# A linear-attention and mixer-MLP kernel on one core: its head reordered (held-back DMA transposes, PE transposes in two PSUM tiles, K chunks finished one by one) and LN1 applied in the Q stage

## The chip, the cores and the metric

The kernel runs on one core of one Trainium2 chip. The metric is the device time of one execution in microseconds (us). A program on one core has no second core to compare with, so every run is read next to runs of the kernel before on the same chip; all runs in this document count as fast ones. PE is the TensorE matmul engine, PEld its weight load, DVE VectorE, ACT ScalarE, POOL GpSimd, SP SyncE (which issues most DMAs).

## The reference, cut to what matters

```python
# x: (1, 2048, 640) bf16; 32 heads of 20
g = sigmoid((x * gate_w).sum(-1, keepdims=True))
# A: linear attention
q, k, v = split_heads(x @ wqkv)
phi = lambda t: where(t > 0, t + 1, exp(t)) + 1e-6
o = phi(q) @ (phi(k)^T v) / (phi(q) . sum(phi(k)) + 1e-6)      # per head
a = merge_heads(o) @ wo
# B: mixer
h  = gelu(layernorm(x) @ w1)                                   # LN1
x1 = x + shift_quarters(h) @ w2
b  = x1 + gelu(layernorm(x1) @ w3) @ w4
out = g * a + (1 - g) * b
```

## The kernel before

Tokens come in 16 chunks of 128. The stages, in PE's order, are: a *head*, in which x chunks 0 to 2 are transposed on PE (the others come transposed by DMA) and multiplied with the K weights; the *K stage*, in which each chunk's K becomes `pk = phi(K)` and is multiplied into the product G = x^T pk; the *Q stage* (ten Q groups, with the rest of G between them); then `w1`, `kv`, `w2`, `w3`, `w4`. PSUM is four tiles `PP[0..3]` of 1024 f32 columns, used in halves of 512, and handed round by `alloc` and `release` in first-in first-out order.

Loads and POOL's work, in program order (cut):

```python
for dc in (0, 1, 2, 4):
    load_wk(aq, dc)                      # K weights, issued from ACT
load_x(0, 1); load_x(1, 2); load_x(2, 3) # plain x chunks, issued from SP
load_wk(sp, 3)
load_xT(3, 4)                            # DMA transposes from here on
load_xT(4, 5); load_x(3, 4); load_xT(5, 7); load_x(4, 6); load_xT(7, 9)
load_x(6, 9); load_xT(9, 12); load_x(9, 12); load_xT(12, 16); load_x(12, 16)
sp.dma_start(wq, ...); sp.dma_start(w1, ...); sp.dma_start(wv, ...)   # [cut: wo6, w2]
# [cut: POOL memsets and masks]
for g in range(4):                       # POOL: waits for the load of w1
    nc.gpsimd.tensor_copy(w1x4[:, :, g, :], w1g[:, :, g, P:CG])
```

phi, LN1 and the head:

```python
def ln1_sq(c):                           # sum of squares on ACT, every 4th chunk the rest on POOL
    act(junk[:], x_sb[:, c, :], ACT.Square, accum_out=sq[:, c:c + 1])
    if c % 4 == 3:
        ...                              # [cut: four small POOL operations: me, ve, sq, ve]
        nc.gpsimd.tensor_tensor(rs1[:, g], ve[:, g], nhalf[:], op=ALU.pow)

def ln1_apply(c):                        # DVE, then a DMA transpose into lnxT
    nc.vector.tensor_scalar(lx[:], x_sb[:, c, :], me[:, c:c + 1], rs1[:, c:c + 1], ...)
    sp.dma_start_transpose(lnxT[:, :, c * P:(c + 1) * P], lx[:])

def phi(dst, src, n, extra=None):        # one ACT exp, two DVE operations
    act(e[:, 0:n], src, ACT.Exp)
    if extra is not None: act(extra[0], extra[1], ACT.Copy)
    nc.vector.tensor_scalar(e[:, 0:n], e[:, 0:n], 1.0, 1e-6, op0=ALU.min, op1=ALU.add)
    nc.vector.scalar_tensor_tensor(dst, src, 0.0, e[:, 0:n], op0=ALU.max, op1=ALU.add)  # L272

for _ in range(5):                       # warm-up
    mm(PP[3][:, 512:1024], lhsT=warm[:, 0:P], rhs=warm[:], start=True, stop=True)
tb = [PP[3][:, 0:512].bitcast(BF16), PP[3][:, 512:1024].bitcast(BF16)]

def x_tr(c, b):
    for dc in range(DC):
        nc.tensor.transpose(tb[b][:, dc * P:(dc + 1) * P], x_sb[:, c, dc * P:(dc + 1) * P], ident[:])
    v = tb[b][:, 0:DC * P].rearrange("p (j s) -> p j s", j=DC)
    nc.vector.tensor_copy(xT[:, 0:3, c * P:(c + 1) * P], v[:, 0:3])
    act(xT[:, 3:5, c * P:(c + 1) * P], v[:, 3:5], ACT.Copy)

x_tr(0, 0)
nc.tensor.transpose(tb[1][:, 0:DC], g5[0:DC, :], ident[0:DC, 0:DC])    # the gate row
for dc in range(DC):
    nc.vector.tensor_copy(wkg[:, dc, D:D + 1], tb[1][:, dc:dc + 1])    # 5 small copies
x_tr(1, 1)
k_mm(0, 0, 0); k_mm(0, 0, 1)
x_tr(2, 0)
k_mm(1, 1, 0); k_mm(1, 1, 1); k_mm(2, 2, 0); k_mm(2, 2, 1)
for dc in range(2, DC):
    for c in range(3):
        k_mm(c, c, dc)
        if dc == DC - 1:
            k_post(c, c)                 # phi, release
for c in range(3, NCH):                  # K stage
    p = alloc()
    for dc in range(DC): k_mm(c, p, dc)
    k_post(c, p)
    g_unit(0, c - 3)
    if c % 2 == 0: pop(ln1_s)
    if c >= 12:    pop(ln1_a)            # LN1 apply of chunks 0 to 3
```

Of the kernel before, what the change touches and what calls it, by code (L numbers as in the profile page):

```python
# [8 lines left out]
ACT = mybir.ActivationFunctionType  # L9
ALU = mybir.AluOpType  # L10
BF16 = mybir.dt.bfloat16
# [5 lines left out]
def kernel(  # L17
# [13 lines left out]
    nc = tc.nc  # L31
    P = 128
    S, D = A_x.shape[1], A_x.shape[2]
# [3 lines left out]
    DC = D // P  # L37
    GW = 120
    gsz = [GW] * 5 + [D - 5 * GW]
# [3 lines left out]
    CG = D // 4  # L43
# [4 lines left out]
    out2 = out.rearrange("b s d -> (b s) d")  # L48
# [4 lines left out]
    def sb(name, cols, dt=BF16):  # L53
        return const.tile([P, cols], dt, name=name)
# [7 lines left out]
    xT = RXT[:].rearrange("p (j s) -> p j s", j=DC)  # L62
# [7 lines left out]
    x_sb = RXH[:, 0:NCH * D].rearrange("p (c d) -> p c d", c=NCH)  # L70
# [4 lines left out]
    wkg = RA[:, 0:DC * KP].rearrange("p (j d) -> p j d", j=DC)  # L75
    o_ = DC * KP
    wq = RA[:, o_:o_ + DC * D].rearrange("p (j d) -> p j d", j=DC)
    o_ += DC * D
    wv = RA[:, o_:o_ + DC * D].rearrange("p (j d) -> p j d", j=DC)
    w3 = RA[:, 0:DC * F].rearrange("p (j f) -> p j f", j=DC)  # L80
    w1 = RB[:, 0:DC * D].rearrange("p (j d) -> p j d", j=DC)
    wo6 = RB[:, DC * D:DC * D + 6 * D].rearrange("p (g d) -> p g d", g=6)
# [3 lines left out]
    w2 = sb("w2", DC * D)[:].rearrange("p (j d) -> p j d", j=DC)  # L86
# [13 lines left out]
    w1x = sb("w1x", DC * P)[:].rearrange("p (j d) -> p j d", j=DC)  # L100
    kvT = sb("kvT", 6 * GW)[:].rearrange("p (g d) -> p g d", g=6)
    warm = sb("warm", 512)
    ident = sb("ident", P)
    ones32 = sb("ones32", 32)
    c32 = sb("c32", 1)
    mask4 = sb("mask4", P)
    mask32 = mask4[:, 0:32]
    E4 = sb("E4", P)
    bmask = sb("bmask", GW, F32)
    g5 = sb("g5", P)  # L110
# [23 lines left out]
    PP = [psum.tile([P, 1024], F32, name=f"pp{i}") for i in range(4)]  # L134
    free = [0, 1, 2, 3]

    def alloc():
        return free.pop(0)

    def release(i):  # L140
        free.append(i)

    mm = nc.tensor.matmul
    act = nc.scalar.activation
# [5 lines left out]
    sp, aq = nc.sync, nc.scalar  # L150
    xv = x2.rearrange("(c p) d -> p c d", p=P)

    def load_x(c0, c1):
        sp.dma_start(x_sb[:, c0:c1, :], xv[:, c0:c1, :])  # L154

    def load_xT(c0, c1):
        sp.dma_start_transpose(xT[:, :, c0 * P:c1 * P], x2[c0 * P:c1 * P, :])  # L157
# [5 lines left out]
    def load_wk(q, dc):  # L163
        q.dma_start(wkg[:, dc, 0:D], A_wqkv[dc * P:(dc + 1) * P, D:2 * D])
# [4 lines left out]
    load_x(1, 2)  # L169
    load_x(2, 3)  # L170
    load_wk(sp, 3)
    load_xT(3, 4)
    load_xT(4, 5)
    load_x(3, 4)
    load_xT(5, 7)
    load_x(4, 6)
    load_xT(7, 9)
    load_x(6, 9)
    load_xT(9, 12)
    load_x(9, 12)  # L180
    load_xT(12, 16)
    load_x(12, 16)
    rows = lambda w, a, b: w[:, a:b].rearrange("(j p) d -> p j d", p=P)
    sp.dma_start(wq, rows(A_wqkv, 0, D))
    sp.dma_start(w1, rows(B_w1, 0, D))
    sp.dma_start(wv, rows(A_wqkv, 2 * D, 3 * D))
    sp.dma_start(wo6[0:GW, 0:5, :], A_wo[0:5 * GW, :].rearrange("(g r) d -> r g d", r=GW))
    sp.dma_start(wo6[0:gsz[5], 5, :], A_wo[5 * GW:D, :])
    sp.dma_start(w2[:, 0:4, :], B_w2.rearrange("(g c) d -> c g d", c=CG)[0:P])
    for g in range(4):  # L190
        sp.dma_start(w2[32 * g:32 * (g + 1), 4, :], B_w2[CG * g + P:CG * (g + 1), :])


    for dc in range(DC):
        nc.gpsimd.memset(wkg[:, dc, D + 1:D + 2], 1.0)
    nc.gpsimd.memset(ones32[:], 1.0)
# [5 lines left out]
                            pattern=[[-DH, 6], [0, DH]], channel_multiplier=1)  # L202
    nc.gpsimd.affine_select(out=bm3, in_=bm3, compare_op=ALU.is_ge, fill=0.0, base=DH - 1,
                            pattern=[[DH, 6], [0, DH]], channel_multiplier=-1)
    nc.gpsimd.memset(mask4[:], 1.0)
    m4 = mask4[:].rearrange("p (f h) -> p f h", f=4)
    nc.gpsimd.affine_select(out=m4, in_=m4, compare_op=ALU.is_ge, fill=0.0, base=0,
                            pattern=[[0, 4], [-4, 32]], channel_multiplier=1)
    nc.gpsimd.affine_select(out=m4, in_=m4, compare_op=ALU.is_ge, fill=0.0, base=3,
                            pattern=[[0, 4], [4, 32]], channel_multiplier=-1)  # L210
    nc.gpsimd.memset(hsT[:, :, 0:4], 0.0)
    nc.gpsimd.memset(hsT[:, :, S:S + 4], 0.0)
    w1g = w1.rearrange("p k (g c) -> p k g c", c=CG)
    w1x4 = w1x.rearrange("p k (g c) -> p k g c", g=4)
    for g in range(4):
        nc.gpsimd.tensor_copy(w1x4[:, :, g, :], w1g[:, :, g, P:CG])


    def stats(mv, c, src):
# [35 lines left out]
    ln1_a = [lambda c=c: ln1_apply(c) for c in range(NCH)]  # L255

    def pop(q, n=1):
        for _ in range(n):
            if q:
                q.pop(0)()  # L260
# [13 lines left out]
    def k_mm(c, p, dc):  # L274
        for (n0, n1) in ((0, 512), (512, KW)):
            mm(PP[p][:, n0:n1], lhsT=xT[:, dc, c * P:(c + 1) * P], rhs=wkg[:, dc, n0:n1],  # L276
               start=(dc == 0), stop=(dc == DC - 1))

    def k_post(c, p):
        phi(pk[:, c, :], PP[p][:, 0:D], D, (ym[:, c, :], PP[p][:, D:D + 2]))  # L280
        release(p)
# [6 lines left out]
    def g_post(i, p):  # L288
        act(Gp[:, i, :], PP[p][:, 0:D], ACT.Copy)
        release(p)  # L290
# [3 lines left out]
    def g_unit(i, c):  # L294
        if c == 0:
            gp[0] = alloc()
        g_step(i, c, gp[0])
        if c == NCH - 1:
            g_post(i, gp[0])


    for _ in range(5):
        mm(PP[3][:, 512:1024], lhsT=warm[:, 0:P], rhs=warm[:], start=True, stop=True)
    tb = [PP[3][:, 0:512].bitcast(BF16), PP[3][:, 512:1024].bitcast(BF16)]

    def x_tr(c, b):
        for dc in range(DC):
            nc.tensor.transpose(tb[b][:, dc * P:(dc + 1) * P], x_sb[:, c, dc * P:(dc + 1) * P], ident[:])
        v = tb[b][:, 0:DC * P].rearrange("p (j s) -> p j s", j=DC)
        nc.vector.tensor_copy(xT[:, 0:3, c * P:(c + 1) * P], v[:, 0:3])  # L310
        act(xT[:, 3:5, c * P:(c + 1) * P], v[:, 3:5], ACT.Copy)

    for _ in range(3):
        alloc()
    x_tr(0, 0)
    nc.tensor.transpose(tb[1][:, 0:DC], g5[0:DC, :], ident[0:DC, 0:DC])
    for dc in range(DC):
        nc.vector.tensor_copy(wkg[:, dc, D:D + 1], tb[1][:, dc:dc + 1])
    x_tr(1, 1)
    k_mm(0, 0, 0)  # L320
    k_mm(0, 0, 1)
    x_tr(2, 0)
    k_mm(1, 1, 0)
    k_mm(1, 1, 1)
    k_mm(2, 2, 0)
    k_mm(2, 2, 1)
    for dc in range(2, DC):
        for c in range(3):
            k_mm(c, c, dc)
            if dc == DC - 1:  # L330
                k_post(c, c)


    for c in range(3, NCH):
        p = alloc()
        for dc in range(DC):
            k_mm(c, p, dc)
        k_post(c, p)
        g_unit(0, c - 3)
        if c % 2 == 0:  # L340
            pop(ln1_s)
        if c >= 12:
            pop(ln1_a)


    gq = [(0, c) for c in range(NCH - 3, NCH)] + [(i, c) for i in range(1, DC) for c in range(NCH)]
    wqp = wq.rearrange("p k (q j) -> p k j q", j=DC)

    def z_rows():
        p = alloc()  # L350
        nc.tensor.transpose(PP[p][:, 0:64].bitcast(BF16), mask4[:], ident[:])
        act(E4[:], PP[p][:, 0:64].bitcast(BF16), ACT.Copy)
        release(p)
        p = alloc()
        for (n0, n1) in COLS:
            for cc in range(0, NCH, 4):
                for q in range(4):
                    mm(PP[p][32 * q:32 * (q + 1), n0:n1], lhsT=ones32[:], rhs=pk[:, cc + q, n0:n1],
                       start=(cc == 0), stop=(cc == NCH - 4), tile_position=(0, 32 * q), skip_group_check=True)
        act(zsb[:], PP[p][:, 0:D], ACT.Copy)  # L360
        release(p)
        nc.vector.tensor_copy(zhi[:], zsb[:])
        nc.vector.tensor_tensor(zlo[:], zsb[:], zhi[:], op=ALU.subtract)
# [13 lines left out]
    n_ = 0  # L377
    for half in range(2):
        for j in range(DC):
            p = alloc()  # L380
            for dc in range(DC):
                for tt in range(2):
                    t0 = half * 1024 + tt * 512
                    mm(PP[p][:, tt * 512:(tt + 1) * 512], lhsT=wqp[:, dc, j], rhs=xT[:, dc, t0:t0 + 512],  # L384
                       start=(dc == 0), stop=(dc == DC - 1))
            phi(pqT[:, j, half * 1024:(half + 1) * 1024], PP[p][:], 1024)
            release(p)
            pop(ln1_s)
            if n_ in (3, 4, 7, 8):
                pop(ln1_a, 2)  # L390
            for _ in range(6 if n_ == 0 else 5):
                g_unit(*gq.pop(0))
            if n_ == 2:
                z_rows()
            if n_ == 4:
                z_cols()
            n_ += 1
# [136 lines left out]
    for c in range(NCH):  # L534
        a, b = stats(mv2, c, x1(c))
# [64 lines left out]
    def fin(c, p, n0, n1, oc):  # L600
        nc.vector.scalar_tensor_tensor(oc[:, n0:n1], PP[p][:, n0:n1], omg[:, c:c + 1], x1(c)[:, n0:n1],  # L601
                                       op0=ALU.mult, op1=ALU.add)
        sp.dma_start(out2[c * P:(c + 1) * P, n0:n1], oc[:, n0:n1])

    def w4_units(t, i, last):
        cs = [4 * t + i, 4 * t + 4 + i]
# [75 lines left out]
```

## Time and profile before

| | before |
|---|---|
| median of the runs when the prediction was made | 272.24 us (271.51 to 272.30) |
| profiled run | 272.18 us, span 270.5 us |
| first K matmul | 6.53 us |
| first Q matmul | 35.02 us |
| first `w1` matmul | 77.70 us |
| last PE result | 267.30 us |

The page of the kernel before: busy time of each engine, then two rows of the slice table (40 equal slices of 6.8 us; a digit is the busy share in tenths, or the granted TensorE clock in tenths).

```profile
span 270.5 us, 4220 instructions
PE 262.2 (97%) x1698; PEld 136.5 (50%) x1698; DVE 116.0 (43%) x211; ACT 110.7 (41%) x165; POOL 32.9 (12%) x111
PE   5989989999999999999999999999999999999995
PEclk9999999999999999999999999999999999999999
```

PE is the bound. What is to be won lies in the first eight slices, before about 50 us. The next view lists what PE waited for: total us, number of waits, longest. (Two lines are cut: 1.2 us for the warm-up data, 0.2 us for x chunk 0.)

```profile
PE pp L316 <- ACT RXT L311: 0.9, 1, 0.9
PE pp L285 <- DVE RPK L272: 0.9, 2, 0.6
PE pp L276 <- DVE RPK L272: 0.8, 1, 0.8
PE pp L308 <- DVE RA L318: 0.5, 1, 0.5
PE pp L384 <- DVE RPK L272: 0.3, 1, 0.3
PE pp L384 <- DVE pqT L272: 0.3, 1, 0.3
```

L308 and L316 are transposes of the head, L276 K, L285 G, L384 Q; L272 is the last operation of phi. The timeline shows the two waits of the head that come first in time (start, duration, engine, line, operation; in brackets the idle time before it and what ended it).

```profile
3.79 0.71 PE L308 MATMUL pp<-ident,RXH 128*128 128x128 bf16 x5 [0.23 <-DMA RXH<-in_A_x_dram]
4.54 0.36 DVE L310 COPY RXT<-pp 128x384 bf16<-128x384 bf16 x1 [3.35 <-PE pp L308]
4.93 0.38 ACT L311 ACTIVATE RXT<-pp 128x256 bf16<-128x256 bf16 x1 [0.99 <-DVE RXT L310]
5.37 0.16 PE L316 MATMUL pp<-ident,g 5*128 5x5 bf16 x1 [0.86 <-ACT RXT L311]
6.04 0.69 PE L308 MATMUL pp<-ident,RXH 128*128 128x128 bf16 x5 [0.51 <-DVE RA L318]
```

DVE's and ACT's copies of one half of a PSUM tile run one after the other (ACT's starts at 4.93, DVE's ended at 4.90), and the gate row, which goes to the *other half* of the same tile, waits for ACT's end at about 5.3. Chunk 1, in that other half too, then waits for the gate row's five copies.

The wait for phi in the first Q group, among the G products:

```profile
38.52 1.25 PE L285 MATMUL pp<-RPK,RXH 128*128 128x512 bf16 x8 [0.64 <-DVE RPK L272]
```

Finally, the speed of a 512-column K matmul in the head: the group of L276 between 6.5 and 8.5 us (count | busy us, mean ns of one | idle).

```profile
L276 PE MATMUL pp<-RA,RXT 128*128 128x512 bf16 x3 | 1.8, 634 | 0.0
```

634 ns is what the profile shows for one of them; in a dense stream they overlap and start every 427 ns. From 8.8 us on they take 379 ns and start every 216 ns. The trace's own record of the granted TensorE clock begins at the same time, at 8.77 us, with full speed. Below, "the clock opens" means this step. The PEclk row of the profile's page does not show it: it is 9 in every slice.

### The profile page before, as it was taken

To read this page: it belongs to the slowest core of one execution; us is meant where nothing else is said; L and a number is where in the kernel's file an instruction comes from. 1 tells how busy PE (TensorE), PEld (TensorE's weight loads), DVE (VectorE), ACT (ScalarE), POOL (GpSimd) and SP (SyncE) were. 2 spreads that over 40 slices of the span, in tenths; PEclk is the share of its full clock that TensorE was granted. 3 is DMA by queue.
4 is the path that set the end of the run, shared out by engine and by line. 5 is a ranking of instruction groups with operands and counts; after the bars stand their busy time and mean duration, and the time that the engine had idled before them with its cause. 6 is when DMAs were issued, how large, how long until landed. Compare 5 with 4: busy or idle time off the path is not lost.

```text
span 270.5 us, 4220 instructions
## 1 busy us (share of the span) xinstructions
PE 262.2 (97%) x1698; PEld 136.5 (50%) x1698; DVE 116.0 (43%) x211; ACT 110.7 (41%) x165; POOL 32.9 (12%) x111
## 2 busy tenths in 40 slices
PE   5989989999999999999999999999999999999995
PEld 2545545555546445555444455555544444555552
DVE  1286583674649044999950023233310001233232
ACT  2356655456542873132978431021134445022020
POOL 5000502011010000344781000000000000000000
PEclk9999999999999999999999999999999999999999
DMA  8999992060351059973563001001000000001001
GB/s 201 235 241 309 294 199 54 0 95 6 73 99 24 2 134 381 347 123 74 47 126 73 0 2 48 27 24 48 27 24 0 0 2 0 24 27 48 26 24 48
DMA packets 42149, 23.95 MB, mean 89 GB/s; under 512 B 30994, under 2 KB 41362, under 8 KB 42130
## 3 DMA queue, kind: packets, MB, share of 16 engines
q1 hardware_dynamic: 41522, 23.03, 35.9%
q10 hardware_dynamic: 576, 0.66, 0.9%
q8 instruction: 13, 0.21, 0.3%
q14 instruction: 6, 0.05, 0.1%
q0 software_dynamic: 32, 0.00, 0.0%
HBM read 12.86 MB, written 3.44 MB: 60 GB/s over the span
## 4 chain that ended last, share of the span: by engine, by line
PE 84%; SPq 6%; DMA 4%; DVE 2%; POOL 1%; issue 1%; ACT 0%; DVEq 0%
PE pp L632 20%; PE pp L565 19%; PE pp L417 8%; PE pp L384 8%; PE pp L591 8%; PE pp L550 8%; PE pp L285 6%; SPq L157 5%; DMA RB<-in_B_w_dram 3%; PE pp L574 2%; PE pp L617 1%; SPq L154 1%; PE pp L626 1%; DMA RA<-in_A_wqkv_dram 1%; PE pp L581 1%; PE pp L451 1%
## 5 line engine op out<-in xcount | busy, mean ns | idle before, releaser
L632 PE MATMUL pp<-RB,RXH 128*128 128x512 bf16 (+1 forms) x390 | 54.4, 299 | 0.0
L565 PE MATMUL pp<-lnxT,RA 128*128 128x512 bf16 x240 | 52.1, 379 | 0.0
L632 PEld LDWEIGHTS <-RXH 128*128 128x128 bf16 x390 | 29.6, 98 | 24.2 <-issue 2.1
L565 PEld LDWEIGHTS <-RA 128*128 128x128 bf16 x240 | 23.4, 98 | 28.1
L567 ACT ACTIVATE RXH<-pp 128x1024 bf16<-128x1024 f32 x24 | 24.3, 1020 | 26.7 <-PE pp L565 26.7
L594 ACT ACTIVATE RXH<-pp,g_all 128x640 f32<-128x640 f32 x16 | 12.7, 794 | 54.9 <-PE pp L591 54.9
L268 ACT ACTIVATE eb<-pp 128x640 bf16<-128x640 f32 (+1 forms) x26 | 21.4, 828 | 27.6 <-PE pp L384 17.9
L285 PE MATMUL pp<-RPK,RXH 128*128 128x512 bf16 (+1 forms) x160 | 25.6, 299 | 0.9 <-DVE RPK L272 0.9
L276 PE MATMUL pp<-RA,RXT 128*128 128x512 bf16 (+1 forms) x160 | 25.0, 307 | 0.8 <-DVE RPK L272 0.8
L384 PE MATMUL pp<-RXT,RA 128*128 128x512 bf16 x100 | 23.2, 379 | 0.6 <-DVE RPK L272 0.3
L591 PE MATMUL pp<-Mp,pqT 128*128 128x512 bf16 (+1 forms) x160 | 23.1, 299 | 0.0
L596 DVE SCALAR_TENSOR_TENSOR RPK<-RPK,omg,RXH 128x640 f32<-128x640 f32 x8 | 7.1, 885 | 36.5 <-ACT RXH L594 36.5
L550 PE MATMUL pp<-w,RXH 128*128 128x512 bf16 (+1 forms) x160 | 21.9, 299 | 0.0
L285 PEld LDWEIGHTS <-RXH 128*128 128x128 bf16 x160 | 12.8, 98 | 11.5 <-issue 1.1
L417 PE MATMUL pp<-lnxT,RB 128*128 128x512 bf16 x80 | 18.3, 380 | 0.0
L276 PEld LDWEIGHTS <-RXT 128*128 128x128 bf16 x160 | 12.8, 100 | 10.4 <-issue 1.4
L271 DVE TENSOR_SCALAR eb<-eb 128x640 bf16<-128x640 bf16 (+1 forms) x26 | 9.5, 365 | 19.4 <-ACT eb L268 19.4
L596 DVE SCALAR_TENSOR_TENSOR RXT<-RXT,omg,RXH 128x640 f32<-128x640 f32 x8 | 7.1, 884 | 24.6 <-ACT RXH L594 24.6
L591 PEld LDWEIGHTS <-pqT 128*128 128x128 bf16 x160 | 12.2, 98 | 10.0 <-issue 0.8
L550 PEld LDWEIGHTS <-RXH 128*128 128x128 bf16 x160 | 12.3, 98 | 9.5
L384 PEld LDWEIGHTS <-RA 128*128 128x128 bf16 x100 | 11.2, 117 | 9.6 <-issue 0.7
L601 DVE SCALAR_TENSOR_TENSOR RXH<-pp,omg,RXT 128x640 bf16<-128x640 f32 x8 | 7.1, 884 | 19.8 <-PE pp L632 19.8
(109 smaller groups left out, 238.1 us busy)
## 6 DMA issues: line engine op xcount, KB each, us to landing
out_dram<-RXH SPq DMA_DIRECT2D x15, 160.0 KB, 1.8
RA<-in_B_w_dram SPq DMA_DIRECT2D x5, 432.0 KB, 6.9
RA<-in_A_wqkv_dram SPq DMA_DIRECT2D x2, 800.0 KB, 9.4
RB<-in_B_w_dram SPq DMA_DIRECT2D x1, 1120.0 KB
RXH<-in_A_x_dram SPq DMA_DIRECT2D x2, 480.0 KB, 4.3
RB<-in_B_w_dram SPq DMA_DIRECT2D x1, 960.0 KB, 12.4
RB<-in_B_w_dram SPq DMA_DIRECT2D x1, 800.0 KB, 8.5
Mp<-Mscr SPq DMA_DIRECT2D x1, 800.0 KB
```

The source lines that it names most:

```text
L157: sp.dma_start_transpose(xT[:, :, c0 * P:c1 * P], x2[c0 * P:c1 * P, :])
L268: act(e[:, 0:n], src, ACT.Exp)
L276: mm(PP[p][:, n0:n1], lhsT=xT[:, dc, c * P:(c + 1) * P], rhs=wkg[:, dc, n0:n1], start=(dc == 0), stop=(dc == DC - 1))
L285: mm(PP[p][:, n0:n1], lhsT=x_sb[:, c, i * P:(i + 1) * P], rhs=pk[:, c, n0:n1], start=(c == 0), stop=(c == NCH - 1))
L384: mm(PP[p][:, tt * 512:(tt + 1) * 512], lhsT=wqp[:, dc, j], rhs=xT[:, dc, t0:t0 + 512], start=(dc == 0), stop=(dc == DC - 1))
L417: mm(PP[p][:, tt * 512:(tt + 1) * 512], lhsT=lh, rhs=lnxT[:, dc, t0:t0 + 512], start=(dc == 0), stop=(dc == DC - 1))
L550: mm(PP[p][:, n0:n1], lhsT=hsT[:, fc, 2 + c * P:2 + (c + 1) * P], rhs=w2[:, fc, n0:n1], start=(fc == 0), stop=(fc == DC - 1))
L565: mm(PP[p][:, k * 512:(k + 1) * 512], lhsT=w3[:, dc, (fc + k) * P:(fc + k + 1) * P], rhs=lnxT[:, dc, t * 512:(t + 1) * 512], start=(dc == ...
L567: act(h2T[:, t % 2, fc:fc + 2, :], PP[p][:].rearrange("p (k s) -> p k s", k=2), ACT.Gelu_apprx_tanh)
L591: mm(PP[p][:, n0:n1], lhsT=pqT[:, j, c * P:(c + 1) * P], rhs=Mp[:, j, n0:n1], start=(j == 0), stop=(j == DC - 1))
L596: nc.vector.scalar_tensor_tensor(x1(c), x1(c), omg[:, c:c + 1], ga, op0=ALU.mult, op1=ALU.add)
L632: mm(PP[p][:, n0:n1], lhsT=h2T[:, k, fc, cc], rhs=w4[:, fc, n0:n1], start=False, stop=(fc == NF - 1))
```

## The change

Its intent: let PE start earlier and without gaps, and take work off the engines that make it wait at the end of the K stage. The diff, cut to its core:

```diff
-    load_xT(3, 4)
-    load_xT(4, 5)
     ... (all later loads, and POOL's four w1x copies, move into late_loads(), same order)
+    # POOL: mask4 is now built first, right after the identity
-        if c >= 12:
-            pop(ln1_a)                                # LN1 applies leave the K stage
...
-    for _ in range(5):
+    for _ in range(6):
         mm(PP[3][:, 512:1024], lhsT=warm[:, 0:P], rhs=warm[:], start=True, stop=True)
+    nc.tensor.transpose(PP[0][:, 0:64].bitcast(BF16), mask4[:], ident[:])   # was in z_rows()
+    act(E4[:], PP[0][:, 0:64].bitcast(BF16), ACT.Copy)
-    def x_tr(c, b):                                   # one tile
+    def x_tr(c, a, b):                                # DVE reads PP[a], ACT reads PP[b]
+            t, k = (ta, dc) if dc < 3 else (tb, dc - 3)
-    x_tr(0, 0)
+    x_tr(0, 3, 2)
+    nc.vector.memset(xT[:, 0, 3 * P:3 * P + 1], 0.0)  # late_loads' first DMA must wait for it
+    late_loads()
+    x_tr(1, 1, 2)                                     # before the gate row, not after it
...
-    for dc in range(2, DC):
-        for c in range(3):
-            k_mm(c, c, dc)
-            if dc == DC - 1:
-                k_post(c, c)
+    for c in range(3):
+        k_mm(c, c, 2)
+    for c in range(3):
+        for dc in (3, 4):
+            k_mm(c, c, dc)
+        k_post(c, c)
...
-        g_unit(0, c - 3)
+        for k in {5: (0, 1), 6: (2, 3), 7: (4,)}.get(c, (c - 3,) if c > 5 else ()):
+            g_unit(0, k)
...
-            if n_ in (3, 4, 7, 8):
+            if n_ in (1, 2, 3, 4, 7, 8):
                 pop(ln1_a, 2)                         # in the Q groups
...
-        sp.dma_start(out2[c * P:(c + 1) * P, n0:n1], oc[:, n0:n1])
+        (aq if n0 else sp).dma_start(out2[c * P:(c + 1) * P, n0:n1], oc[:, n0:n1])
```

More of the change, by code (lines that the diff above doesn't have):

```diff
@@ L171 @@
     load_wk(sp, 3)
-    load_xT(3, 4)
-    load_xT(4, 5)
-    load_x(3, 4)
-    load_xT(5, 7)
-    load_x(4, 6)
-    load_xT(7, 9)
-    load_x(6, 9)
-    load_xT(9, 12)
-    load_x(9, 12)
-    load_xT(12, 16)
-    load_x(12, 16)
-    rows = lambda w, a, b: w[:, a:b].rearrange("(j p) d -> p j d", p=P)
-    sp.dma_start(wq, rows(A_wqkv, 0, D))
-    sp.dma_start(w1, rows(B_w1, 0, D))
-    sp.dma_start(wv, rows(A_wqkv, 2 * D, 3 * D))
-    sp.dma_start(wo6[0:GW, 0:5, :], A_wo[0:5 * GW, :].rearrange("(g r) d -> r g d", r=GW))
-    sp.dma_start(wo6[0:gsz[5], 5, :], A_wo[5 * GW:D, :])
-    sp.dma_start(w2[:, 0:4, :], B_w2.rearrange("(g c) d -> c g d", c=CG)[0:P])
-    for g in range(4):
-        sp.dma_start(w2[32 * g:32 * (g + 1), 4, :], B_w2[CG * g + P:CG * (g + 1), :])
+    nc.gpsimd.memset(mask4[:], 1.0)
+    m4 = mask4[:].rearrange("p (f h) -> p f h", f=4)
+    nc.gpsimd.affine_select(out=m4, in_=m4, compare_op=ALU.is_ge, fill=0.0, base=0,
+                            pattern=[[0, 4], [-4, 32]], channel_multiplier=1)
+    nc.gpsimd.affine_select(out=m4, in_=m4, compare_op=ALU.is_ge, fill=0.0, base=3,
+                            pattern=[[0, 4], [4, 32]], channel_multiplier=-1)
     for dc in range(DC):
@@ L204 @@
                             pattern=[[DH, 6], [0, DH]], channel_multiplier=-1)
-    nc.gpsimd.memset(mask4[:], 1.0)
-    m4 = mask4[:].rearrange("p (f h) -> p f h", f=4)
-    nc.gpsimd.affine_select(out=m4, in_=m4, compare_op=ALU.is_ge, fill=0.0, base=0,
-                            pattern=[[0, 4], [-4, 32]], channel_multiplier=1)
-    nc.gpsimd.affine_select(out=m4, in_=m4, compare_op=ALU.is_ge, fill=0.0, base=3,
-                            pattern=[[0, 4], [4, 32]], channel_multiplier=-1)
     nc.gpsimd.memset(hsT[:, :, 0:4], 0.0)
     nc.gpsimd.memset(hsT[:, :, S:S + 4], 0.0)
-    w1g = w1.rearrange("p k (g c) -> p k g c", c=CG)
-    w1x4 = w1x.rearrange("p k (g c) -> p k g c", g=4)
-    for g in range(4):
-        nc.gpsimd.tensor_copy(w1x4[:, :, g, :], w1g[:, :, g, P:CG])
     def stats(mv, c, src):
@@ L299, in g_unit, with late_loads @@
             g_post(i, gp[0])
-    for _ in range(5):
+    def late_loads():
+        load_xT(3, 4)
+        load_xT(4, 5)
+        load_x(3, 4)
+        load_xT(5, 7)
+        load_x(4, 6)
+        load_xT(7, 9)
+        load_x(6, 9)
+        load_xT(9, 12)
+        load_x(9, 12)
+        load_xT(12, 16)
+        load_x(12, 16)
+        rows = lambda w, a, b: w[:, a:b].rearrange("(j p) d -> p j d", p=P)
+        sp.dma_start(wq, rows(A_wqkv, 0, D))
+        sp.dma_start(w1, rows(B_w1, 0, D))
+        sp.dma_start(wv, rows(A_wqkv, 2 * D, 3 * D))
+        sp.dma_start(wo6[0:GW, 0:5, :], A_wo[0:5 * GW, :].rearrange("(g r) d -> r g d", r=GW))
+        sp.dma_start(wo6[0:gsz[5], 5, :], A_wo[5 * GW:D, :])
+        sp.dma_start(w2[:, 0:4, :], B_w2.rearrange("(g c) d -> c g d", c=CG)[0:P])
+        for g in range(4):
+            sp.dma_start(w2[32 * g:32 * (g + 1), 4, :], B_w2[CG * g + P:CG * (g + 1), :])
+        w1g = w1.rearrange("p k (g c) -> p k g c", c=CG)
+        w1x4 = w1x.rearrange("p k (g c) -> p k g c", g=4)
+        for g in range(4):
+            nc.gpsimd.tensor_copy(w1x4[:, :, g, :], w1g[:, :, g, P:CG])
@@ L303 @@
+    for _ in range(6):
         mm(PP[3][:, 512:1024], lhsT=warm[:, 0:P], rhs=warm[:], start=True, stop=True)
-    tb = [PP[3][:, 0:512].bitcast(BF16), PP[3][:, 512:1024].bitcast(BF16)]
-    def x_tr(c, b):
+    nc.tensor.transpose(PP[0][:, 0:64].bitcast(BF16), mask4[:], ident[:])
+    act(E4[:], PP[0][:, 0:64].bitcast(BF16), ACT.Copy)
+    def x_tr(c, a, b):
+        ta, tb = PP[a][:, 0:512].bitcast(BF16), PP[b][:, 0:512].bitcast(BF16)
         for dc in range(DC):
-            nc.tensor.transpose(tb[b][:, dc * P:(dc + 1) * P], x_sb[:, c, dc * P:(dc + 1) * P], ident[:])
-        v = tb[b][:, 0:DC * P].rearrange("p (j s) -> p j s", j=DC)
-        nc.vector.tensor_copy(xT[:, 0:3, c * P:(c + 1) * P], v[:, 0:3])
-        act(xT[:, 3:5, c * P:(c + 1) * P], v[:, 3:5], ACT.Copy)
+            t, k = (ta, dc) if dc < 3 else (tb, dc - 3)
+            nc.tensor.transpose(t[:, k * P:(k + 1) * P], x_sb[:, c, dc * P:(dc + 1) * P], ident[:])
+        nc.vector.tensor_copy(xT[:, 0:3, c * P:(c + 1) * P], ta[:, 0:3 * P].rearrange("p (j s) -> p j s", j=3))
+        act(xT[:, 3:5, c * P:(c + 1) * P], tb[:, 0:2 * P].rearrange("p (j s) -> p j s", j=2), ACT.Copy)
@@ L313 @@
     for _ in range(3):
         alloc()
-    x_tr(0, 0)
-    nc.tensor.transpose(tb[1][:, 0:DC], g5[0:DC, :], ident[0:DC, 0:DC])
+    x_tr(0, 3, 2)
+    nc.vector.memset(xT[:, 0, 3 * P:3 * P + 1], 0.0)
+    late_loads()
+    x_tr(1, 1, 2)
+    tg = PP[3][:, 512:1024].bitcast(BF16)
+    nc.tensor.transpose(tg[:, 0:DC], g5[0:DC, :], ident[0:DC, 0:DC])
     for dc in range(DC):
-        nc.vector.tensor_copy(wkg[:, dc, D:D + 1], tb[1][:, dc:dc + 1])
-    x_tr(1, 1)
+        nc.vector.tensor_copy(wkg[:, dc, D:D + 1], tg[:, dc:dc + 1])
@@ L320 @@
     k_mm(0, 0, 0)
     k_mm(0, 0, 1)
-    x_tr(2, 0)
+    x_tr(2, 3, 2)
     k_mm(1, 1, 0)
@@ L349, in z_rows @@
     def z_rows():
-        p = alloc()
-        nc.tensor.transpose(PP[p][:, 0:64].bitcast(BF16), mask4[:], ident[:])
-        act(E4[:], PP[p][:, 0:64].bitcast(BF16), ACT.Copy)
-        release(p)
         p = alloc()
```

## The prediction

> **What bounds the kernel.** Page of the kernel before: PE is busy 262.2 of 270.5 us (97%), the chain of waits is 84% PE. Only three places have anything to win (timeline of PE):
>
> 1. Head (to about 15 us). First x transpose at 3.79. Then PE idles 0.86 us before the gate-row transpose, 0.51 us before chunk 1's transposes (which share a PSUM half with the gate row and wait for its DVE copies), 0.21 and 0.76 us before the first G product and K chunk 4 (both wait for the DVE end of phi, L272: chunks 0 to 2 finish together, so their phis queue at 1.2 us each). ACT's x copy starts only when DVE's copy of the same PSUM tile ended (4.93 after 4.90). x chunk 2, issued at 1.73, lands at 7.38, because DMA transposes, issued from 3.59, run beside the first loads.
> 512-column matmuls start every 427 ns until about 8.7 us, then every 216 ns: [...]
> 2. End of K, start of Q: PE waits for L272 about 0.5 us at 34.5 and 0.8 us at 37.7; DVE lags because four LN1 applies (0.44 us each) sit in the last K chunks. At 48.0 a Q group waits 0.3 us for a PSUM buffer, after the 0.15 us mask transpose.
> 3. Tail: one queue issues the last two output DMAs, at 267.40 and 267.82.
>
> **What the change does.** Transposes wait for a DVE memset behind the first x copy (estimate 5.1 us). The first loads, 1.3 MB, then land by about 6.1 us, x chunk 2 by 5.3. Two PSUM tiles let ACT and DVE copy side by side (0.38 us off each handover) and free chunk 1 of the gate row. K chunks finish one after another and the first G products move behind K chunk 5, so phi hides. It adds a 0.43 us warm-up matmul, ending about when x lands, and moves the mask transpose there (0.1 us). LN1 applies move to Q groups, where DVE idles 1.8 us each.
>
> **The sum.**
> - First K matmul at about 5.6 us rather than 6.53; with the 0.21 and 0.76 us waits gone, K chunk 8 starts 1.7 us earlier if the clock still opens near 8.7 us[...]
> - Q stage: 0.5 + 0.8 + 0.3 + 0.15 = 1.7 us.
> - Tail: 0.1 us.
>
> All of it lies on the PE chain; nothing later has slack to swallow it: 3.5 to 4.7 us at best. Less something for new small waits (gate-column copies before the first K matmuls, later DMA transposes): **268.8 us**, 8 times in 10 within **267.2 to 270.6**. Chances: faster by over 2% 0.10, within 2% 0.89, slower by over 2% 0.01.
>
> **Signs.** Right: x chunk 2 lands near 5.3; K matmuls start before 6 us; no PE wait for the DVE end of phi between 9 and 50 us; Q starts 2 to 3.5 us earlier (before: 35.0), the w1 stage (before: 77.7) 3 to 4.5 us earlier, and that lead is kept. Whether the 216 ns spacing starts near 5 or 8.7 us decides between the halves of my range.
>
> **What would make it wrong.** Held-back transposes land late: the piece for chunks 12 to 15 landed at 23.7 and was needed at 28.0; it may come 1.5 us later and be needed 3 us sooner. If K chunks 3, 5 or 12 wait for it, the gain shrinks to the Q part. [...]

The head's part of the sum came in two branches, of which one is K chunk 8 2.9 us earlier if the clock opened sooner, to which the author gave half a chance. With the Q stage's 1.7 us and the tail's 0.1 us the sum came to 3.5 us (with the 1.7 us) or 4.7 us (with the 2.9 us). That the clock would open so much sooner was the estimate; no trace then at hand showed it.

## More of the kernel before

One more stretch of this timeline, from the end of the K stage, was looked at too lightly in the prediction, as will be seen:

```profile
29.90 1.20 POOL L216 COPY w1x<-RB 128x160 bf16<-128x160 bf16 x4 [24.95 <-DMA RB<-in_B_w_dram]
32.24 1.05 POOL L246 TENSOR_TENSOR rs<-ve,nhalf 128x4 f32<-128x4 f32 x1
33.33 0.45 DVE L250 TENSOR_SCALAR lnxs<-RXH,me,rs 128x640 bf16<-128x640 bf16 x1 [1.71 <-POOL rs L246]
34.14 0.82 DVE L272 SCALAR_TENSOR_TENSOR RPK<-pp,eb 128x640 bf16<-128x640 f32 x1
35.02 0.81 PE L384 MATMUL pp<-RXT,RA 128*128 128x512 bf16 x3 [0.33 <-DVE RPK L272]
```

## The result, and the profile after

| | before | after | lead |
|---|---|---|---|
| median | 272.21 us (4 runs, 271.51 to 272.30) | 267.93 us (4 runs, 267.62 to 268.17) | 4.28 |
| span of the profiled run | 270.47 us | 266.46 us | 4.01 |
| first K matmul | 6.53 us | 5.41 us | 1.12 |
| K chunk 8 starts | 21.45 us | 18.29 us | 3.16 |
| K chunk 9 starts | 23.09 us | 20.78 us | 2.31 |
| first Q matmul | 35.02 us | 32.23 us | 2.79 |
| first `w1` matmul | 77.70 us | 73.74 us | 3.96 |
| last PE result | 267.30 us | 263.34 us | 3.96 |

The ratio of after to before is 0.9848, with a 95% interval from 0.9827 to 0.9868: 1.5% faster, inside the 2% that the verdict calls the same, but clear of noise. Ratios in this document are the mean time of one kernel's fast runs over that of the other's fast runs of the same rounds, so not quite the ratio of the medians.

The waits of PE after the change, all of them:

```profile
PE pp L305 <- DVE warm L159: 1.2, 1, 1.2
PE pp L252 <- DMA RXT<-in_A_x_dram: 0.7, 1, 0.7
PE pp L635 <- issue: 0.3, 2, 0.2
```

Every wait of the first list is gone. The first line is the warm-up's and was there before; L635 is a matmul of the last stage (0.3 us). One wait is new and lies in the K stage: K (now L252) waited once for a DMA transpose. The timeline shows where, at chunk 9:

```profile
19.65 0.43 PE L261 MATMUL pp<-RPK,RXH 128*128 128x512 bf16 x2
20.78 1.48 PE L252 MATMUL pp<-RA,RXT 128*128 128x512 bf16 x9 [0.69 <-DMA RXT<-in_A_x_dram]
```

The head's timeline: ACT's copy (L315) now starts before DVE's ends, and all ten transposes of chunks 0 and 1 merge into one row without the gate row between them.

```profile
3.89 1.48 PE L313 MATMUL pp<-ident,RXH 128*128 128x128 bf16 x10
4.46 0.36 DVE L314 COPY RXT<-pp 128x384 bf16<-128x384 bf16 x1 [3.26 <-PE pp L313]
4.67 0.38 ACT L315 ACTIVATE RXT<-pp 128x256 bf16<-128x256 bf16 x1 [0.25 <-PE pp L313]
5.30 0.17 PE L324 MATMUL pp<-ident,g 5*128 5x5 bf16 x1
5.41 0.82 PE L252 MATMUL pp<-RA,RXT 128*128 128x512 bf16 x4
```

And the K matmuls between 5.4 and 8.4 us, to set against the 634 ns of before:

```profile
L252 PE MATMUL pp<-RA,RXT 128*128 128x512 bf16 x10 | 3.1, 380 | 0.0
```

They ran at the fast clock (380 ns, against 379 ns after 8.8 us in the kernel before). The transposes' spacing drops from 107 to 56 ns at about 4.6 us, against 8.8 us before.

A ledger of the 4.01 us in the spans, from the table: 3.16 us won by K chunk 8; 0.85 us lost at chunk 9 (the lead falls from 3.16 to 2.31; the view's idle time of 0.69 us counts from the end of the G products before, and where nothing waits K starts 0.16 us ahead of that end, as at 21.45 us in the trace of before); 1.65 us won from there to `w1` (2.31 to 3.96); nothing lost after `w1`; 0.05 us at the tail. The tail's output-queue edit is too small to test.

### The profile page after: what moved, and what is told of

The parts are those of the page before. It is cut to its first block, busy times and chain, and to the rows that moved or that the text cites. A ratio compares the mean times of both kernels' runs of the same rounds, so it can differ in the third digit from the quotient of the medians.

```text
span 266.5 us, 4191 instructions
## 1 busy us (share of the span) xinstructions
PE 259.3 (97%) x1666; PEld 135.6 (51%) x1699; DVE 116.0 (44%) x212; ACT 110.8 (42%) x165; POOL 32.8 (12%) x111
## 4 chain that ended last, share of the span: by engine, by line
PE 91%; DMA 3%; SPq 2%; issue 1%; DVE 1%; ACT 0%
PE pp L635 20%; PE pp L568 19%; PE pp L420 8%; PE pp L594 8%; PE pp L387 8%; PE pp L553 8%; PE pp L261 8%; PE pp L252 4%; DMA RXT<-in_A_x_dram 3%; PE pp L577 2%; SPq L157 2%; PE pp L620 1%; PE pp L629 1%; PE pp L305 1%; PE pp L584 1%
## 5 line engine op out<-in xcount | busy, mean ns | idle before, releaser
L635 PE MATMUL pp<-RB,RXH 128*128 128x128 bf16 (+1 forms) x381 | 53.5, 297 | 0.7 <-issue 0.3
L635 PEld LDWEIGHTS <-RXH 128*128 128x128 bf16 x390 | 29.7, 98 | 24.2 <-issue 2.1
L261 PE MATMUL pp<-RPK,RXH 128*128 128x128 bf16 (+1 forms) x157 | 25.0, 297 | 0.2
L252 PE MATMUL pp<-RA,RXT 128*128 128x512 bf16 (+1 forms) x157 | 23.8, 298 | 0.8 <-DMA RXT<-in_A_x_dram 0.7
L599 DVE SCALAR_TENSOR_TENSOR RPK<-RPK,omg,RXH 128x640 f32<-128x640 f32 x8 | 7.1, 885 | 36.5 <-ACT RXH L597 36.5
L553 PE MATMUL pp<-w,RXH 128*128 128x128 bf16 (+1 forms) x157 | 21.7, 297 | 0.2
L252 PEld LDWEIGHTS <-RXT 128*128 128x128 bf16 x160 | 12.3, 98 | 10.4 <-DMA RXT<-in_A_x_dram 1.0
L387 PEld LDWEIGHTS <-RA 128*128 128x128 bf16 x100 | 11.1, 118 | 8.9
```

Source lines behind the costliest of these rows:

```text
L252: mm(PP[p][:, n0:n1], lhsT=xT[:, dc, c * P:(c + 1) * P], rhs=wkg[:, dc, n0:n1], start=(dc == 0), stop=(dc == DC - 1))
L261: mm(PP[p][:, n0:n1], lhsT=x_sb[:, c, i * P:(i + 1) * P], rhs=pk[:, c, n0:n1], start=(c == 0), stop=(c == NCH - 1))
L387: mm(PP[p][:, tt * 512:(tt + 1) * 512], lhsT=wqp[:, dc, j], rhs=xT[:, dc, t0:t0 + 512], start=(dc == 0), stop=(dc == DC - 1))
L553: mm(PP[p][:, n0:n1], lhsT=hsT[:, fc, 2 + c * P:2 + (c + 1) * P], rhs=w2[:, fc, n0:n1], start=(fc == 0), stop=(fc == DC - 1))
L599: nc.vector.scalar_tensor_tensor(x1(c), x1(c), omg[:, c:c + 1], ga, op0=ALU.mult, op1=ALU.add)
L635: mm(PP[p][:, n0:n1], lhsT=h2T[:, k, fc, cc], rhs=w4[:, fc, n0:n1], start=False, stop=(fc == NF - 1))
```

## The experiments

Twelve kernels ran, in three groups of four on a chip each, 5 rounds each (4 to 6 runs of a kernel). All results were correct. "vs. before" is the ratio to the runs of the kernel before in the same group (11 runs each; medians 272.41, 272.01 and 272.08 us). "Clock opens" is the time in the one profiled run at which matmuls change from the slow to the fast spacing, read from its trace; the packed trace's record of the granted clock, which begins at 8.77 us in before and at 4.49 us in after, agrees with the change of spacing to about 0.1 us there.

| kernel | median us | vs. before (95%) | clock opens, us |
|---|---|---|---|
| no_hold | 267.65 | 0.9828 (0.9804 to 0.9852) | 4.0 |
| swap_loads | 267.86 | 0.9832 (0.9810 to 0.9854) | 5.7 |
| no_warmup | 269.14 | 0.9868 (0.9845 to 0.9891) | 9.6 |
| ln1_in_k | 274.23 | 1.0067 (1.0038 to 1.0096) | 5.7 |
| after_again | 267.96 | 0.9845 (0.9824 to 0.9866) | 5.2 to 5.7 |
| ln1_in_k_w1x_late | 268.14 | 0.9846 (0.9824 to 0.9868) | 5.7 |
| k_together | 268.88 | 0.9878 (0.9856 to 0.9899) | 4.8 to 5.1 |
| before_w1x_late | 272.29 | 0.9999 (0.9978 to 1.0019) | 10.3 |
| before_k_order | 272.45 | 1.0007 (0.9989 to 1.0026) | 11.1 |
| before_k_order_ln1_q | 270.17 | 0.9924 (0.9907 to 0.9941) | 9.2 |
| before_ln1_in_q | 272.16 | 0.9976 (0.9948 to 1.0004) | 12.0 |
| one_psum | 268.24 | 0.9865 (0.9841 to 0.9889) | 9.1 |

### no_hold: the DMA transposes not held back

```diff
-    nc.vector.memset(xT[:, 0, 3 * P:3 * P + 1], 0.0)
-    late_loads()
+    late_loads()          # moved up, in front of the warm-up
     for _ in range(6):
```

> The changed kernel without the hold-back: the DVE memset is gone and the DMA transposes are issued right behind the first loads, as before the change. Theory A (the hold-back mainly moves a wait: it lets x chunk 2 land at 6.0 instead of 7.4 us, but costs the new wait of K chunk 9 for its transposed x, 0.69 us in the trace): chunk 2's PE transposes wait about 1.3 us near 6.1 us, K chunk 9 waits for nothing, net 0.3 to 0.7 us slower than the changed kernel, about 268.4. Rival B (the hold-back is the core of the gain): slower by 2 us or more, about 270 or above. Rival C (it is not needed): equal or faster than 267.9.

It was 267.65 us, so rival C holds: nothing is lost without the hold-back, and at this resolution nothing is clearly won (0.9828 against 0.9848 and 0.9845 of the changed kernel). Theory A's premise, that chunk 2 lands late without it, did not come true. Here is the line of the x loads issued before 2.2 us (chunks 0 to 2), issue to landing; the largest is chunk 2's. First the kernel before, in which transposes follow directly:

```profile
DMA to landing us min/median/max: 2.9/3.3/5.7
```

no_hold, in which they also follow directly:

```profile
DMA to landing us min/median/max: 2.8/3.1/4.3
```

after_again, in which they are held back:

```profile
DMA to landing us min/median/max: 2.9/3.2/4.6
```

And ln1_in_k_w1x_late, held back by the same memset:

```profile
DMA to landing us min/median/max: 3.0/3.3/5.4
```

Issued at 1.72 to 1.74 us in all 14 traces, chunk 2 took 4.3 to 5.7 us in the six whose transposes follow directly (first transpose issued at 3.6 to 4.0 us) and 4.0 to 5.4 us in the eight that hold them back (4.75 to 5.1 us). The medians, 4.9 and 4.4 us, differ by 0.5 us, but the two ranges overlap almost wholly: a small effect of the hold-back is neither shown nor excluded, and most of the spread is between runs. The 7.38 us landing that the prediction explained by the transposes was the latest of these draws.

### swap_loads: the transpose for chunks 9 to 11 in front of the plain load of chunks 6 to 8

```diff
-        load_x(6, 9)
-        load_xT(9, 12)
+        load_xT(9, 12)
+        load_x(6, 9)
```

> The changed kernel with the DMA transpose for chunks 9 to 11 issued before the plain load of x chunks 6 to 8. Theory A (K chunk 9 waits for that transpose because 480 KB of plain x stand before it): the 0.69 us wait goes, the G product of chunk 6 finds its x just landed, and the kernel is 0.5 to 0.9 us faster than the changed one, about 267.2. Rival B (the transposes are bound by the rate of their own packets or by later backlog): the wait moves to the G product of chunk 6 or to K chunk 12, and nothing or less than 0.3 us is won.

It was 267.86 us. In its trace PE waits for nothing but the warm-up data (and 0.3 us in the last stage), so the 0.69 us wait is gone and has not moved. But the time is that of after_again (0.9832 against 0.9845), whose own trace has no wait at chunk 9 either. The wait of the first trace is real but not there in every run: chunk 9's transposed x came at about 20.7 us there, and PE wants it at about 20. Theory A's mechanism fits, its 0.5 to 0.9 us gain does not; that the swap removed the wait is not shown, since after_again lost it without the swap.

### no_warmup: PE's first work is the mask transpose

```diff
-    for _ in range(6):
+    for _ in range(0):
         mm(PP[3][:, 512:1024], lhsT=warm[:, 0:P], rhs=warm[:], start=True, stop=True)
```

> The changed kernel without its six warm-up matmuls; the mask transpose is then the first PE work, near 3.7 us. Theory A ([...]): the 56 ns spacing of transposes and the 216 ns spacing of 512-column matmuls start between 7 and 10.6 us, and the kernel is 1.0 to 2.5 us slower, 268.9 to 270.4. Rival B (the head is bound by loads and handovers, the clock hardly matters): less than 0.4 us slower. Rival C ([...] warm-ups or not): opening near 4.6 us in this run too.

It was 269.14 us, 1.2 us over the changed kernel's median and 1.0 us over swap_loads of the same group (0.0036 of 272). Its K matmuls between 5.4 and 9.4 us:

```profile
L252 PE MATMUL pp<-RA,RXT 128*128 128x512 bf16 x7 | 3.9, 626 | 0.0
```

The clock opened at 9.6 us (7 to 10.6 was the estimate), against about 4.6 us with the warm-up (the first trace), and Q started at 33.18 instead of 31.68 us (after_again). Theory A, that the early opening comes with the warm-up's PE work from 1.25 us on, holds, at its low end.

### ln1_in_k: the LN1 applies back in the K stage

```diff
         if c % 2 == 0:
             pop(ln1_s)
+        if c >= 12:
+            pop(ln1_a)
...
-            if n_ in (1, 2, 3, 4, 7, 8):
+            if n_ in (3, 4, 7, 8):
```

> The changed kernel with the first four LN1 applies back in K chunks 12 to 15. Theory A (they delay the phis on DVE, and PE waits for that at the end of K and in the first Q group): the two waits on the DVE end of phi come back, about 0.5 us before Q and 0.8 us before the third G product of the first Q group; 1.2 us slower than the changed kernel, about 269.1. Rival B (those waits came from the early G products and the late start of the phis, not from LN1): within 0.3 us of the changed kernel.

It was 274.23 us: about 6 us slower than the changed kernel, and slower than the kernel *before*. Neither theory allowed for that. The timeline:

```profile
31.22 1.11 POOL L301 COPY w1x<-RB 128x160 bf16<-128x160 bf16 x4 [26.28 <-DMA RB<-in_B_w_dram]
33.47 1.05 POOL L222 TENSOR_TENSOR rs<-ve,nhalf 128x4 f32<-128x4 f32 x1
34.55 0.45 DVE L226 TENSOR_SCALAR lnxs<-RXH,me,rs 128x640 bf16<-128x640 bf16 x1 [5.59 <-POOL rs L222]
36.24 4.00 PE L389 MATMUL pp<-RXT,RA 128*128 128x512 bf16 x10 [4.17 <-DVE RPK L248]
```

DVE stands idle for 5.59 us at the first LN1 apply. It waits for `rs1`, which POOL computes; in POOL's program the four `w1x` copies come first, and they wait for the load of `w1` (landed at 31.16 us): POOL runs the copies at 31.22 us and the last step of `rs1` at 33.47 us. Every phi behind the apply waits as well: no phi passes the waiting apply in this trace, and DVE's next phi operation starts at 34.91 us, behind the apply. So PE's Q waits 4.17 us for a PSUM tile. Then the ten Q matmuls take 4.00 us rather than the 2.32 us of other Q groups: after the gap the clock is slow again from 36.5 to about 39.9 us. Here the page of the run does show it, as a 7 in the sixth slice:

```profile
PEclk9999979999999999999999999999999999999999
```

The mean granted clock of all six runs of ln1_in_k is 0.988 to 0.994, against 0.998 to 1.000 in the changed kernel's runs, so the estimate is that the clock was slow again for a while in each of them (one was traced); the two runs at 0.988 are also the two slowest.

The same chain, only shorter, is in the trace of the kernel before (1.71 us at 33.33). So the four applies themselves, at 0.44 us of DVE each, may not have been the cause at all. A new theory: Q is *pinned* to the landing of `w1`.

### ln1_in_k_w1x_late: applies in K, but POOL's copies behind the K loop

```diff
 # ln1_in_k, and:
-        for g in range(4):
-            nc.gpsimd.tensor_copy(w1x4[:, :, g, :], w1g[:, :, g, P:CG])   # at the end of late_loads()
+    for g in range(4):
+        nc.gpsimd.tensor_copy(w1x4[:, :, g, :], w1g[:, :, g, P:CG])       # behind the K loop
```

> The first four LN1 applies in K chunks 12 to 15 (that alone gave 274.2 us), but the four POOL copies into w1x, which wait for the load of w1, are put behind the K loop in POOL's order. Theory A (the applies wait on DVE for POOL's rs1, POOL waits in order for the w1 load, and every later phi stands behind them): DVE's 5.6 us wait and PE's 4.2 us wait before Q vanish, within 0.4 us of the changed kernel, about 267.9 to 268.3. Theory B, that of the prediction (the applies cost DVE 0.44 us each, and that alone makes PE wait): the waits before Q stay, at 0.5 and 0.8 us, about 269.2. Theory C (something else in POOL's or SP's order): near 274.

It was 268.14 us, ratio 0.9846, the same as the changed kernel. Theory A holds and theory B, the prediction's, falls: with the applies in the K stage but POOL free, Q does not wait. All the waits of PE in its trace, and its first Q group, which has none:

```profile
PE pp L301 <- DVE warm L159: 1.2, 1, 1.2
PE pp L309 <- DMA RXH<-in_A_x_dram: 0.9, 1, 0.9
32.51 2.32 PE L390 MATMUL pp<-RXT,RA 128*128 128x512 bf16 x10
```

The 0.9 us is a wait for x chunk 2, which fits this run's 268.45 us, the slowest of its five.

### after_again: the changed kernel once more

> The changed kernel once more, unedited, as the yardstick of this group and as a second look at its head. Expected 267.6 to 268.3. [...] K chunk 9 may or may not wait for its transposed x (0.69 us in the first trace, 0.06 us in a relative).

It was 267.96 us, as expected. The clock opened between 5.2 and 5.7 us, later than in the first trace (about 4.6), and K chunk 9 did not wait.

### k_together: the first K chunks finished together again, first G products early

```diff
-    for c in range(3):
-        k_mm(c, c, 2)
-    for c in range(3):
-        for dc in (3, 4):
-            k_mm(c, c, dc)
-        k_post(c, c)
+    for dc in range(2, DC):
+        for c in range(3):
+            k_mm(c, c, dc)
+            if dc == DC - 1:
+                k_post(c, c)
...
-        for k in {5: (0, 1), 6: (2, 3), 7: (4,)}.get(c, (c - 3,) if c > 5 else ()):
-            g_unit(0, k)
+        g_unit(0, c - 3)
```

> The changed kernel with the first three K chunks finished together and the first G products right behind chunks 3, 4, 5, as before. Theory A: PE waits for the DVE end of phi before the first G product and K chunk 4 come back, about 0.2 and 0.8 us; part of it is given back because K chunk 9's wait for its transposed x shrinks; 0.5 to 1.0 us slower than the changed kernel. Rival B (the earlier end of the head hides phi already): within 0.3 us.

It was 268.88 us, 0.9 us over after_again of the same group. Both waits are back:

```profile
PE pp L252 <- DVE RPK L248: 0.8, 1, 0.8
PE pp L261 <- DVE RPK L248: 0.2, 1, 0.2
```

Theory A holds; the sum of the waits (1.0 us) is about the loss.

### before_w1x_late: one edit of the kernel before

```diff
 # the kernel before
-    for g in range(4):
-        nc.gpsimd.tensor_copy(w1x4[:, :, g, :], w1g[:, :, g, P:CG])
...
+    for g in range(4):                       # behind the K loop
+        nc.gpsimd.tensor_copy(w1x4[:, :, g, :], w1g[:, :, g, P:CG])
```

> The kernel before with one edit: the four POOL copies into w1x behind the K loop; LN1 applies stay in K. Theory A (the waits at the end of K were POOL's, which stood behind the w1 load): both waits, 0.5 and 0.8 us, go; 1.0 to 1.4 us faster than before. Theory B (DVE time of the applies): no faster than before by more than 0.3 us.

It was 272.29 us, ratio 0.9999. The mechanism of theory A came true, its gain did not. The trace has no wait at the end of K: PE's K work ends at 35.21 and Q starts at 35.32 us. But K itself ended 0.8 us later than in the trace of before (34.42), because here the clock opened at 10.3 instead of 8.8 us. The kernel before does not show such a delay in its total, because there Q waits anyway. So, as this one trace reads, a pin hides gains and losses of everything in front of it, and taking away the pin alone is worth only what the head happens to have in hand; the other five runs were not traced. The next three runs test the idea.

### before_k_order, before_ln1_in_q, before_k_order_ln1_q: one, the other, both

The K-order edit is that of the diff above, the LN1 edit too; nothing else is taken from the change.

> The kernel before, with only the order of K and G changed: chunks 0 to 2 finished one by one, first G products behind chunk 5; LN1 applies still in K. Theory A (the start of Q is pinned to the landing of the w1 load through POOL's copies, POOL's rs1 and DVE): the 0.2 and 0.8 us waits near 14 us go, the wait before Q grows by as much, Q still starts near 35 us, nothing won (within 0.4 us of before), although the head ends 1 us sooner. Rival B (gains of the head and of LN1 add up): 0.8 to 1.0 us faster than before.

> The kernel before with only the LN1 applies moved to the Q groups. The edit of POOL's order, which freed the same waits, gave 0.9999 of before. Theory A (with the clock opening late, near 10 us, the head is so late that the pin hardly costs): within 0.6 us of before, 271.5 to 272.2. The prediction's ledger: 1.3 us faster, about 270.8.

> The same edit of the kernel before plus the LN1 applies moved to the Q groups. Theory A: nothing pins Q, so the head's 1 us reaches the end, together with what the moved applies give: 1.0 to 2.2 us faster than before, and 1 us or more faster than with the order alone. Rival B (additive): about 1.0 us faster than before from the order, and as much as the LN1 move gives alone on top.

| edit of the kernel before | vs. before | as us of 272.1 (95%) |
|---|---|---|
| K order alone | 1.0007 | +0.2 (-0.3 to +0.7) |
| LN1 applies to Q alone | 0.9976 | -0.7 (-1.4 to +0.1) |
| both | 0.9924 | -2.1 (-2.5 to -1.6) |

The edits are not additive: -0.5 us as a sum, -2.1 us together, a difference clear of the intervals. Theory A holds for the K order and for both together. For the LN1 edit alone it is open: the interval takes in no gain at all and the prediction's 1.3 us alike. In before_k_order the waits near 14 us are gone, and Q starts at 35.10 us (before: 35.02), again one step behind the same chain:

```profile
32.32 1.05 POOL L246 TENSOR_TENSOR rs<-ve,nhalf 128x4 f32<-128x4 f32 x1
33.41 0.45 DVE L250 TENSOR_SCALAR lnxs<-RXH,me,rs 128x640 bf16<-128x640 bf16 x1 [1.45 <-POOL rs L246]
34.22 0.82 DVE L272 SCALAR_TENSOR_TENSOR RPK<-pp,eb 128x640 bf16<-128x640 f32 x1
35.10 2.32 PE L386 MATMUL pp<-RXT,RA 128*128 128x512 bf16 x10 [0.15 <-DVE RPK L272]
```

In that run the clock opened at 11.1 us, 2.3 us later than in the run of before, and the span is the same to 0.1 us (270.55 and 270.47): the pin took it up. (So the head did not end 1 us sooner in this run, and the wait before Q did not grow as theory A has it; it fell to 0.15 us.) Without the pin the time follows the head: the six runs of before_ln1_in_q spread from 270.26 to 272.64 us, and the one profiled, with the clock opening at 12.0 us, was the slowest.

### one_psum: the PE transposes in halves of one tile again

```diff
-    def x_tr(c, a, b):
-        ta, tb = PP[a][:, 0:512].bitcast(BF16), PP[b][:, 0:512].bitcast(BF16)
+    tb = [PP[3][:, 0:512].bitcast(BF16), PP[3][:, 512:1024].bitcast(BF16)]
+    def x_tr(c, b):      # as in the kernel before
...
-    x_tr(0, 3, 2) ... x_tr(1, 1, 2) ... tg = PP[3][:, 512:1024] ... x_tr(2, 3, 2)
+    x_tr(0, 0)    ... x_tr(1, 1)    ... tg = PP[2][:, 512:1024] ... x_tr(2, 0)
```

> The changed kernel with the PE transposes of x in two halves of one PSUM tile again (the gate row goes to another tile). Theory A (an access to any part of the tile waits for the last reader of the whole tile): ACT's copies start after DVE's, chunk 1's transposes wait for ACT's copy of chunk 0 to about 5.35 us, chunk 2's to about 6.7 us; first K matmul 0.3 us later, K chunk 3 0.5 to 0.9 us later, 0.4 to 1.0 us slower than the changed kernel, about 268.3 to 268.9[...]. Rival B (loads bound the head, x chunk 2 lands near 6.3 anyway): within 0.3 us.

It was 268.24 us in the median, but in two clusters: 268.13 to 268.24 (four runs) and 269.40 and 269.88. The profiled run is of the slow cluster:

```profile
5.06 0.38 ACT L316 ACTIVATE RXT<-pp 128x256 bf16<-128x256 bf16 x1 [0.65 <-DVE RXT L321]
5.49 0.69 PE L313 MATMUL pp<-ident,RXH 128*128 128x128 bf16 x5 [0.86 <-ACT RXT L316]
6.24 1.26 PE L252 MATMUL pp<-RA,RXT 128*128 128x512 bf16 x3
```

Chunk 1's transposes, which write the other half of the tile, wait 0.86 us for ACT's last read of the first half; the first K matmul comes 0.8 us later than in the changed kernel's first trace. ACT's copy, too, starts only when DVE's copy of the same half has ended (at 5.03; L321 is the memset right behind it). With two tiles, in the trace of after, the copies overlap: DVE's runs from 4.46 to 4.82 us, ACT's starts at 4.67. So theory A's handover is shown in the trace; whether the hardware or the program's bookkeeping per tile asks for the 0.86 us, no run separates. In the total its cost is not clear of noise (0.9865 against 0.9848, intervals overlapping). In this run the clock, too, opened late, at 9.1 us, against about 4.6 us in the changed kernel's first trace; what of the cost is the clock's and what the gap's, no run separates. That the four faster runs had an early opening is the estimate; they were not traced.

## Why the prediction was right, and where it was not

The predicted total, 268.8 us in a range of 267.2 to 270.6, holds the measured 267.93 us, and the chance was put on "within 2%". Point by point:

- **Head: right in its parts.** The first K matmul was put at about 5.6 us and came at 5.41. K chunk 8 was to be 1.7 or 2.9 us early, depending on the clock, and was 3.16 us early. The waits on phi are gone, and k_together shows that the new order is what removed them in the head (0.9 us). one_psum shows the handover of PSUM tiles.
- **Clock: the early branch.** Given half a chance; the clock opened at 4.0 to 5.8 us in all six further traces that kept both the warm-up and the two-tile handover, as in the first. no_warmup shows its worth, about 1.0 to 1.2 us. This is why the result lies in the faster half of the range.
- **"x chunk 2 by 5.3", thanks to the hold-back: wrong.** The transposes were held as planned (first one issued at 4.86 us), but chunk 2 landed at 6.00 us, and in no_hold at 5.97 us without holding anything back. The prediction took one slow landing (7.38 us) for an effect of the transposes.
- **"DVE lags because four LN1 applies (0.44 us each) sit in the last K chunks": wrong mechanism, right size by luck.** The luck is that the edit takes the applies out of the K stage, which removes the measured waits whichever mechanism made them. The wait was DVE's for POOL's `rs1`, behind copies that wait for the load of `w1`: ln1_in_k_w1x_late has the applies in place and no loss. The trace of before already said so (`1.71 <-POOL rs L246`); the prediction named the engine that PE waited for and did not ask what that engine waited for.
- **"Q stage: 1.7 us": measured 1.65 us** from K chunk 9 to `w1`. Its last two terms (0.3 us for a PSUM buffer, 0.15 us for the mask transpose) are in this sum, but no run tests them apart. Of the tail's 0.1 us, 0.05 us is seen.
- **A plain sum of head and Q gains: right for the whole change, wrong as an idea.** In the kernel before the terms are not independent. Had the change left the LN1 applies where they were, it would have been 1.8 us slower than the kernel before (ln1_in_k, ratio 1.0067): its better head could not pass the pin, `w1` landed later (31.16 against 29.84 us, with the loads held back; not tested apart), and behind the long wait the clock was slow again (1.7 us in the first Q group). The LN1 move alone is worth about 0.7 us, if anything. Only together do they give 4.1 us (0.9848 and 0.9845 of 272).
- **"New small waits": one came.** Of the risk named, a K chunk waiting for a held-back transpose, chunk 9 paid 0.85 us in one of the eight traces with the hold-back, came 0.2 us late in ln1_in_k, and not at all late in the others.

No version beats the changed kernel beyond doubt. no_hold, which has less code, is at least its equal.

## What to carry to other kernels

When an engine on the critical path waits for a second engine, follow the second engine's own wait to its end: here it led from PE over DVE and POOL to a DMA, and reordering POOL's four copies cured a wait that looked like too much DVE work (ln1_in_k against ln1_in_k_w1x_late, 6 us). Where a stage is pinned to something late and outside, gains before the pin are swallowed and edits can't be judged one at a time; try them in pairs. One trace is one draw: a landing time or a clock opening that differs by 1 to 3 us between traces of the same head, as here, is no evidence for a mechanism until a second run shows it.

## What the traces show of the clock, the transposes and the landings

- The opening comes at different times. With the first matmul at 1.25 us and few gaps it came 2.7 to 4.6 us after it (opening at 4.0 to 5.8); in heads with gaps of 0.5 to 0.9 us, 7.5 to 10.8 us (8.8 to 12.0); in no_warmup, whose PE starts at 3.69 us, 5.9 us (9.6). The same head opened at about 4.6 us (after) and between 5.2 and 5.7 us (after_again). How much PE work it takes to open the clock, these runs do not show.
- In ln1_in_k the slow clock followed a gap of 4.17 us, but not at once: the first two matmuls behind the gap still start 215 ns apart, and the 427 ns spacing follows, from 36.5 to about 39.9 us.
- The profile's page hides the opening: its PEclk row is 9 throughout in both kernels, because the trace's record of the clock begins only at the opening (8.77 us in before, 4.49 us in after). The later slow stretch does show (the 7 in ln1_in_k).
- SP was held 1.3 us for issuing a DMA transpose of 128 rows of 640, 1.3 to 1.4 us for 256 and 4.5 us for 512, against 0.58 us for a plain load (the trace of after; what part of it is waiting is not shown).
- The same 160 KB load, issued at 1.7 us, took 4.0 to 5.7 us to land over the 14 traces (5.7 in before, 4.3 in after).
